# Linear attention with a mixture-of-experts layer: values ahead of state products in the first and last block pairs, and other moves in the order of the attention stage

## The chip, the cores and the metric

The kernel runs on one core of a Trainium2 chip. The metric is the time of one execution on the device in microseconds (us). The kernel before took 392.94 us as the median of three runs, which lay between 392.67 and 392.99 us.

A core has engines that work side by side and wait for one another through semaphores: PE (TensorE, matrix products; each of its products is preceded by a weight load), DVE (VectorE), ACT (ScalarE), POOL (GpSimd) and SP (SyncE, which here only issues transfers). Each engine works through its own instructions in order. Products land in PSUM, from which DVE and ACT read.

## The reference

Queries, keys and values have shape (4 batches, 8 heads, 768 positions, 64). The first half is linear attention with decay, computed in blocks; the second half sends each of the 3072 rows of 512 numbers to one of 8 experts.

```
for each block b of the sequence:
    intra = (q_b k_b^T) * Dmask          # Dmask[i,j] = lam^(i-j) for i >= j
    out_b = intra v_b + (q_b * lam^(pos+1)) kv_state
    kv_state = lam^block * kv_state + (k_b * lam^(block-1-pos))^T v_b
x = out as 3072 rows of 512
e = argmax(x w_gate + modality_bias);  p = its probability
out[row] = p * (relu(x[row] w1[e]) w2[e])
```

## The kernel before, in words

**Blocks.** The kernel takes blocks of 128 positions, so each batch has NC = 6 blocks and there are 24 blocks, g = 0 to 23. They are loaded in pairs: load(m) brings k, q, v and k by rows for blocks 2m and 2m+1, into one of four slots. A load into a used slot waits until the products that read it are done. The first two pairs come in four transfers each, so that PE can begin early.

**The steps of one block.** `scores(g)` (line 250) are 16 products on PE into the PSUM tile s; `mask(g)` multiplies them by the decay matrix dk on DVE and gives the tile pt. `query(g)` (line 218) makes q times the powers pq on POOL. `keys(g)` (line 226) makes the decayed keys kd, in 8 instructions on ACT, or in one on POOL where on_pool is set. `products(g)` (line 263) are 16 products on PE that make the block's share of the state, into one half of the PSUM tile kv: even blocks write its first half, odd blocks its second. `add(g)` (line 272) adds that share to the decayed state on DVE; for the first block of a batch it is one copy. `from_state(both)` (line 283) opens an output tile o for each block named and multiplies the state before the block by the decayed query; its products use half of the array's rows and half of its columns each, and where two blocks are named their products alternate. `values(g)` (line 294) adds pt times v to the same tile o, closes it, and copies it on ACT into xt, which gathers four blocks. The tile o has two buffers, s has two, kv has one.

**Turning and gating.** Four blocks in xt make a group. `turn(grp, tb)` transposes a quarter of it on PE into a buffer of o, and DVE and then ACT copy it out as rows. `gates(grp)` are 32 small products that give the routing scores. `turns(grp)` (line 333) is turn, turn, gates, turn, turn.

**The order.** For PE, DVE, ACT and SP the order of the instructions is the order in which the program calls them; nothing is moved. The opening (lines 813 to 856) is written out by hand for blocks 0 to 5. Then a loop runs over m = 2 to 11, called pass m here: with a = 2m and b = 2m+1 it does add(b), the scores, masks, keys and queries of blocks a+2 and b+2, some small routing steps, the state products and values of blocks a and b, then products(a+2), products(b+2), add(a+2), and in odd passes the four turns. Pass 2 handles block 5 alone, since the opening has already finished block 4. The loop begins thus:

```
for m in range(2, pairs):
    a, b = HB * m, HB * m + 1
    ahead = m + 1 < pairs
    add(b)
    ...
    if ahead:
        block(a + 2)
        mm = block(b + 2)
```

`keep_busy(n)` (line 788) issues n products whose result nobody reads. Small DVE steps (choosing the expert, the lists of tiles) are put into a list by `put`, and `do(n)` issues the next n of them. `tick(mm)` lets one scatter of finished rows go out on POOL after the product mm.

**The experts.** After the loop, wide tiles of 256 rows run through the experts (`first_layer`, `second`). Two thin tiles, of 64 and of 32 rows, are worked in between: `thin_second` (line 750) is a thin tile's second layer, its scaling on ACT and its output transfer by POOL. It is called inside the `first_layer` of the next wide tile through `finish`. The last wide tile's second layer ends the kernel.

Of the kernel before, what the change touches and what calls it, by code (L numbers as in the profile page):

```python
# [15 lines left out]
P = 128  # L16
B, H, S, D = 4, 8, 768, 64
NP = H // 2
# [25 lines left out]
def linear_attention_moe(tc, qkv, lam, modality, wg, mbias, w1, w2, out):  # L44
    nc = tc.nc
    with ExitStack() as ctx:
# [163 lines left out]
        def loaded(g):  # L210

            t = halves[g // HB][:, :, g % HB]
            kt, qt = (t[:, i].rearrange("p (a t) -> p a t", a=NP) for i in range(2))
            return kt, qt, t[:, 2], t[:, 3]
# [65 lines left out]
                                                   scalar=pq[:, p, P - 1 : P], in1=kp[:, g % HB, p, :],  # L280
                                                   op0=ALU.mult, op1=ALU.add)

        def from_state(both):

            for g in both:
                ops[g] = ps.tile([P, NP, P], F32, name="o", bufs=2)
            for p in range(NP):
                for g in both:
                    if g % NC > 0:
                        for hl, r in enumerate(halves2):  # L290
                            nc.tensor.matmul(ops[g][place(g, hl), p, :], state[g % NC % 3][r, p, :], qds[g][r, p, :],  # L291
                                             start=(p == 0), stop=False)

        def values(g):
            c = g % NC
            vt, op, pt = loaded(g)[2], ops.pop(g), pts.pop(g)
            for p in range(NP):
                for hl in range(2):
                    mm = nc.tensor.matmul(op[place(g, hl), p, :], vt[:, (2 * p + hl) * D : (2 * p + hl + 1) * D],  # L299
                                          pt[:, hl, p, :], start=(c == 0 and p == 0), stop=(p == NP - 1))  # L300
            if g % 4 == 0:
                xts[g // 4] = work.tile([P, NP, 4, 4, Q], F32, name="xt", bufs=2)
            nc.scalar.copy(out=xts[g // 4][:, :, :, ORDER.index(g % 4), :], in_=op.rearrange("p a (c t) -> p a c t", c=4))
            return mm

        groups = []
# [8 lines left out]
        def turn(grp, tb):  # L315
            tp = ps.tile([P, NP, P], F32, name="o", bufs=2)
            for p in range(NP):
                nc.tensor.transpose(out=tp[:, p, :], in_=xts[grp][:, p, tb].rearrange("k t a -> k (t a)"), identity=ident)  # L318
            row = row_tile(4 * grp + tb)[:, :DM].rearrange("t (p h d) -> t p h d", p=NP, h=2)
            tp = tp.rearrange("t p (h d) -> t p h d", h=2)  # L320
            half = P // 2
            nc.vector.tensor_copy(out=row[:half], in_=tp[:half])
            for h in range(2):
                nc.scalar.copy(out=row[half:, :, h], in_=tp[half:, :, 1 - h])

        def gates(grp):
            for p in range(NP):
                for t in range(4):
                    mm = nc.tensor.matmul(lps[t * Q : (t + 1) * Q, grp % 2, :], wgq[:, ORDER[t] % HB, p, :], xts[grp][:, p, :, t, :],
                                          start=(p == 0), stop=(p == NP - 1), tile_position=(0, t * Q))  # L330
            return mm

        def turns(grp):
            turn(grp, 0)
            turn(grp, 1)
            mm = gates(grp)
            turn(grp, 2)
            turn(grp, 3)
            return mm
# [102 lines left out]
        def count():  # L442

            nc.tensor.matmul(cp, onesb, ohsum, start=True, stop=True)
# [367 lines left out]

        keep_busy(9)
        decays()
        keys(0, True)
        scores(0)
        mask(0)
        keep_busy(5)
        lam_halves()
        powers()  # L820
        from_state((0,))
        values(0)
        block(1, True)
        products(0)
        add(0)
        block(2)
        keys(3)
        from_state((1,))
        values(1)
        products(1)  # L830
        add(1)
        scores(3)
        mask(3)
        query(3)
        products(2)
        gpsimd_constants()
        load(SLOTS)
        from_state((2,))
        values(2)
        add(2)  # L840
        products(3)
        from_state((3,))
        values(3)
        add(3)
        block(4)
        turn(0, 0)
        turn(0, 1)
        gates(0)
        block(5)
        turn(0, 2)  # L850
        turn(0, 3)
        load(1 + SLOTS)
        products(4)
        add(4)
        from_state((4,))
        values(4)
        for m in range(2, pairs):
            a, b = HB * m, HB * m + 1
            ahead = m + 1 < pairs
            add(b)  # L860
            if m == 4 or m == 8:
                routed = m // 4 - 1, *choose(m // 4 - 1, gate_rows())
# [3 lines that stand above are left out]
                if m > 4:  # L866
                    tick(mm)
            if m == 2:
                routing_constants()
            elif m == 3:  # L870
                clear(slice(E * CAP, E * CAP + TT), TT)
            do(9 if m % 4 == 0 else 8)
            if m > 2:
                from_state((a, b))
                values(a)
            else:
                from_state((b,))
            mm = values(b)
            if m == 5 or m == 9:
                jobs += [("slots", one_slot)] * RC  # L880
            if m > 4:
                tick(mm)
            if m + SLOTS < pairs:
                load(m + SLOTS)
            if ahead:
                for g in (a + 2, b + 2):
                    products(g)
                add(a + 2)
            if m == 4 or m == 8:
                ranks(routed[-1])  # L890
                slots += slots_of(*routed)
            elif m == 5:
                count()
                early = early_list("A", listA)
            elif m == 9:
                count()
                early = early_list("B", listB, early)
            elif m == 10:
                turn_rows(0)
            if m % 2 and ahead:  # L900
                mm = turns(m // 2)
                if m > 4:
                    tick(mm)
            else:
                do(4)
            if m == 8:
                need("slots")
                raw1 = w1_part("raw1", F32)
                fetch_w1(*fetch_regs(0, True))
                fetch_x(0)  # L910
            elif m == 9:
                raw2 = w2_part("raw2", F32)
                fetch_w2(*fetch_regs(0, True))
                fetch_x(1)
# [97 lines left out]
        for n in [3] + list(range(wides, fixed_ones)):  # L1012
            first_layer(between)
            between = lambda i: None
            thin = {wides + 1: thins, wides + 3: thins + 1}.get(n)
            if thin:
                thin_rows(thin)
            m = n + 1 if n > 3 else wides
            if m < fixed_ones:
                fetch_w2(*fetch_regs(m, m == wides))  # L1020
                turn_rows(m)
                split_rows()
                if m + 1 < fixed_ones:
                    fetch_x(m + 1)
                split_w1()
                if m + 1 < fixed_ones:
                    fetch_w1(*fetch_regs(m + 1))
            second(n, 0)
            if thin:
                hn = thin_first(xf[thin], homes[thin][0])  # L1030
            second(n, 1)
            if thin:
                hnt[thin] = thin_turn(hn)
                between = finish(thin, 0)
            thin = {wides: thins, wides + 2: thins + 1}.get(n)
            if thin:
                fetch_x(thin)
                fetch_w1(*fetch_regs(thin, True), to=homes[thin][0])
                fetch_w2(*fetch_regs(thin, True), to=homes[thin][1])
        ordered.close()  # L1040
        _, (more,) = nc.values_load_multi_w_load_instructions(
            nums[0:1, 0:1], engines=mybir.ALL_ENGINES, min_val=MIN_WIDE, max_val=MAX_WIDE, bass_reorder=False)
# [65 lines left out]
```

## Time and profile before

| what | value |
|---|---|
| runs | 392.67, 392.94, 392.99 us |
| the profiled execution | 393.13 us, of which the span from first to last instruction is 391.4 us |
| PE busy | 381.3 us, 97% of the span, 3602 products |
| DVE, ACT, POOL busy | 66%, 54%, 25% |
| PE in 40 slices of 9.8 us | 8, 9, 8, then 9 in each until the last, which is 3 |
| DMA busy in the same slices | 7 in the first, 9 in the next three, mixed after, 2 or less in most of the last ten |

The profile is of one execution on the core. An engine's busy time is the sum of its instructions. In a row of the timeline the first number is the start, the second how long the row lasts; "x16" says that 16 instructions are merged in it; a bracket says how long the engine was idle before it and which instruction ended that wait. Products are pipelined and their ends are modelled, so one row of PE may overlap the next by some hundredths of a microsecond.

### The profile page before, as it was taken

The page shows a single profiled execution, that of the slowest core. Times are in us where ns is not written, and L with a number is a line of the kernel's source. Part 1 is how long each engine was busy: PE and PEld are TensorE (multiplying, and loading weights), DVE is VectorE, ACT ScalarE, POOL GpSimd, SP SyncE. Part 2 cuts the span into 40 slices and gives each one's busy share as a digit, 9 for nine tenths or more (in the row PEclk, how much of TensorE's full clock was granted, in tenths as well). Part 3 has the DMA queues.
Part 4 walks back from the last instruction along what each step waited for, and adds up shares of the span by engine and source line. Part 5 has one row for each costly group of instructions (what it writes and reads, how often), then busy time and mean ns, then how long its engine had stood idle before and what let it go on. Part 6 is the DMA issues. An engine that isn't in the chain of part 4 may idle for free.

```text
span 391.4 us, 9713 instructions
## 1 busy us (share of the span) xinstructions
PE 381.3 (97%) x3602; PEld 337.5 (86%) x3602; DVE 256.8 (66%) x461; ACT 210.5 (54%) x411; POOL 98.3 (25%) x128
## 2 busy tenths in 40 slices
PE   8989999999999999999999999999999999999993
PEld 4879888898888989999898987889979899898982
DVE  6667779878577687875768574375764756668520
ACT  1558578675556564464746454355355554646520
POOL 1653218656411267020020102102012020201101
PEclk9999999999999999999999999999999999999998
DMA  7999977999759993399814999762950211200101
GB/s 250 388 402 338 360 253 288 383 345 329 232 147 287 332 336 147 140 371 307 245 55 119 289 405 305 269 194 63 337 175 30 56 54 26 56 28 3 55 2 51
DMA packets 42456, 82.72 MB, mean 211 GB/s; under 512 B 7326, under 2 KB 20126, under 8 KB 42400
## 3 DMA queue, kind: packets, MB, share of 16 engines
q1 hardware_dynamic: 38480, 69.23, 53.5%
q0 software_dynamic: 3920, 12.78, 8.5%
q8 instruction: 30, 0.49, 0.5%
q14 instruction: 26, 0.21, 0.2%
HBM read 89.52 MB, written 17.84 MB: 274 GB/s over the span
## 4 chain that ended last, share of the span: by engine, by line
PE 56%; issue 31%; POOL 4%; DMA 3%; DVE 3%; SPq 1%; ACT 1%; POOLq 0%; DVEq 0%
PE o L674 6%; PE o L676 6%; PE o L675 6%; PE s L255 5%; PE o L299 5%; POOL out_dram L718 4%; PE o L291 3%; PE kv L674 2%; PE s L676 2%; PE kv L675 2%; PE s L675 2%; PE s L674 2%; PE kv L676 2%; PE o L318 2%; DMA load<-in_qkv_dram 2%
## 5 line engine op out<-in xcount | busy, mean ns | idle before, releaser
L583 DVE TENSOR_TENSOR w2l<-raw,w2h 128x1024 fp32r<-128x1024 f32 x48 | 58.8, 1224 | 39.2 <-ACT w2h L582 38.1
L718 POOL DMA_INDIRECT out_dram<-y,idx x24 | 30.0, 1249 | 212.2 <-ACT y L717 188.2
L674 PE MATMUL o<-w2h,hh 128*128 128x512 f32 x192 | 75.4, 393 | 0.0
L676 PE MATMUL o<-w2h,hl 128*128 128x512 f32 x192 | 74.9, 390 | 0.0
L675 PE MATMUL o<-w2l,hh 128*128 128x512 f32 x192 | 74.8, 390 | 0.0
L583 DVE TENSOR_TENSOR w1l<-raw,w1h 128x1024 fp32r<-128x1024 f32 x44 | 51.5, 1220 | 2.0 <-ACT w1h L582 2.0
L582 ACT CAST w2h<-raw 128x1024 fp32r<-128x1024 f32 x48 | 49.9, 1039 | 0.0
L674 PE MATMUL kv<-xh,w1h 128*128 128x256 f32 x176 | 49.8, 283 | 0.0
L674 PE MATMUL s<-xh,w1h 128*128 128x256 f32 x176 | 49.6, 282 | 0.0
L675 PE MATMUL s<-xl,w1h 128*128 128x256 f32 x176 | 49.5, 281 | 0.0
L675 PE MATMUL kv<-xl,w1h 128*128 128x256 f32 x176 | 49.5, 281 | 0.0
L676 PE MATMUL s<-xh,w1l 128*128 128x256 f32 x176 | 49.5, 281 | 0.0
L676 PE MATMUL kv<-xh,w1l 128*128 128x256 f32 x176 | 49.5, 281 | 0.0
L582 ACT CAST w1h<-raw 128x1024 fp32r<-128x1024 f32 x44 | 42.9, 1046 | 0.0
L674 PEld LDWEIGHTS o<-w2h,hh 128*128 128x128 f32 x192 | 36.0, 188 | 7.8 <-issue 0.8
L676 PEld LDWEIGHTS o<-w2h,hl 128*128 128x128 f32 x192 | 36.1, 188 | 7.6
L675 PEld LDWEIGHTS o<-w2l,hh 128*128 128x128 f32 x192 | 36.1, 188 | 7.1
L717 ACT ACTIVATE y<-o,idx 128x512 f32<-128x512 f32 x24 | 16.4, 684 | 40.4 <-PE o L676 34.6
L237 ACT ACTIVATE kd<-load,dk 128x64 f32<-128x64 f32 x144 | 35.7, 339 | 3.5 <-DMA load<-in_qkv_dram 3.4
L674 PEld LDWEIGHTS kv<-xh,w1h 128*128 128x128 f32 x176 | 33.3, 189 | 0.6 <-issue 0.6
L674 PEld LDWEIGHTS s<-xh,w1h 128*128 128x128 f32 x176 | 33.2, 189 | 0.3
L675 PEld LDWEIGHTS s<-xl,w1h 128*128 128x128 f32 x176 | 33.2, 189 | 0.3
(190 smaller groups left out, 637.1 us busy)
## 6 DMA issues: line engine op xcount, KB each, us to landing
raw<-in_w_dram SPq DMA_DIRECT2D x96, 512.0 KB
load<-in_qkv_dram SPq DMA_DIRECT2D x6, 2048.0 KB
both<-in_w_dram SPq DMA_DIRECT2D x16, 512.0 KB
xg<-placed SPq DMA_DIRECT2D x48, 128.0 KB
placed<-blank SPq DMA_DIRECT2D x9, 528.0 KB
load<-in_qkv_dram SPq DMA_DIRECT2D x8, 512.0 KB
load<-in_qkv_dram SPq DMA_DIRECT2D x4, 1024.0 KB
load<-in_qkv_dram SPq DMA_DIRECT2D x4, 768.0 KB
```

Of the source, the lines that this page charges most:

```text
L237: nc.scalar.activation(out=kds[g][:, p, hl, :], in_=kn[:, p, hl, :], func=AF.Copy, scale=dk[:, hl, p, P - 1 : P])
L255: mm = nc.tensor.matmul(scs[g][:, hl, p, :], kt[r, p, :], qt[r, p, :], start=True, stop=True)
L291: nc.tensor.matmul(ops[g][place(g, hl), p, :], state[g % NC % 3][r, p, :], qds[g][r, p, :], start=(p == 0), stop=False)
L299: mm = nc.tensor.matmul(op[place(g, hl), p, :], vt[:, (2 * p + hl) * D : (2 * p + hl + 1) * D], pt[:, hl, p, :], start=(c == 0 and p == 0) ...
L318: nc.tensor.transpose(out=tp[:, p, :], in_=xts[grp][:, p, tb].rearrange("k t a -> k (t a)"), identity=ident)
L582: nc.scalar.copy(out=hi, in_=src)
L583: nc.vector.tensor_tensor(out=lo, in0=src, in1=hi.bitcast(F32), op=ALU.subtract)
L674: nc.tensor.matmul(out, ah, bh, start=first, stop=False)
L675: nc.tensor.matmul(out, ah, bl, start=False, stop=False)
L676: return nc.tensor.matmul(out, al, bh, start=False, stop=last)
L717: nc.scalar.activation(out=y, in_=yp, func=AF.Copy, scale=idx[:, t, 1:2].bitcast(F32))
L718: sc = nc.gpsimd.indirect_dma_start(out=out, out_offset=bass.IndirectOffsetOnAxis(ap=idx[:, t, 0:1], axis=0), in_=y, in_offset=None, bound ...
```

## The change

There are five edits.

1. A pair of blocks can now begin its output tiles with `values(g, begins=True)` and end them with `from_state(both, ends=True)`, which then copies both tiles out (`give`). Blocks 2 and 3, 4 and 5, and 22 and 23 are done so; 22 and 23 had been a pair before, in the other order.
2. In the opening `lam_halves` and `powers` stand ahead of the first mask, the five products of `keep_busy(5)` are gone, scores(1) stand ahead of products(0), the keys of block 1 are made on ACT, and load(4) is called ahead of scores(3) instead of behind products(2).
3. In the loop add(a+2) stands between products(a+2) and products(b+2). In odd passes products(b+2) stand inside `turns`, between the gates and the last two turns.
4. In odd passes four small steps (`do(4)`) and, in passes 5 and 9, the start of a list stand inside `turns` as well; the `do(4)` at the end of the even passes is gone, and the rows of a group are scattered one tick later.
5. The second thin tile's `thin_second` comes after the last wide tile.

```
+        def from_state(both, ends=False):
...
-                                             start=(p == 0), stop=False)
+                                             start=(p == 0 and not ends), stop=(ends and p == NP - 1))
+            if ends:
+                for g in both:
+                    give(g)
...
-        def turns(grp):
+        def turns(grp, amid):
             turn(grp, 0)
             turn(grp, 1)
             mm = gates(grp)
+            do(4)
+            amid()
             turn(grp, 2)
             turn(grp, 3)
...
         decays()
+        lam_halves()
+        powers()
         keys(0, True)
         scores(0)
         mask(0)
-        keep_busy(5)
-        lam_halves()
-        powers()
-        from_state((0,))
-        values(0)
-        block(1, True)
+        scores(1)
         products(0)
         add(0)
-        block(2)
-        keys(3)
+        values(0)
+        mask(1)
+        query(1)
+        keys(1)
         from_state((1,))
         values(1)
+        scores(2)
+        mask(2)
+        query(2)
+        keys(2)
         products(1)
         add(1)
+        load(SLOTS)
         scores(3)
         mask(3)
         query(3)
+        keys(3)
+        gpsimd_constants()
         products(2)
-        gpsimd_constants()
-        load(SLOTS)
-        from_state((2,))
-        values(2)
         add(2)
+        values(2, begins=True)
+        values(3, begins=True)
         products(3)
-        from_state((3,))
-        values(3)
+        from_state((2, 3), ends=True)
+        load(1 + SLOTS)
         add(3)
         block(4)
         turn(0, 0)
         turn(0, 1)
         gates(0)
-        block(5)
+        products(4)
         turn(0, 2)
         turn(0, 3)
-        load(1 + SLOTS)
-        products(4)
         add(4)
-        from_state((4,))
-        values(4)
+        block(5)
+        values(4, begins=True)
...
+            if m == 2:
+                mm = values(b, begins=True)
+                from_state((a, b), ends=True)
+            elif not ahead:
+                values(a, begins=True)
+                mm = values(b, begins=True)
+                from_state((a, b), ends=True)
+            else:
                 from_state((a, b))
                 values(a)
...
             if ahead:
-                for g in (a + 2, b + 2):
-                    products(g)
+                products(a + 2)
                 add(a + 2)
             if m == 4 or m == 8:
+                products(b + 2)
                 ranks(routed[-1])
...
-            if m % 2 and ahead:
-                mm = turns(m // 2)
+            elif m % 2 and ahead:
+                def amid():
+                    begin_list()
+                    products(b + 2)
+                mm = turns(m // 2, amid)
...
-            else:
-                do(4)
+            elif ahead:
+                products(b + 2)
...
-                between = finish(thin, 0)
+                if thin == thins:
+                    between = finish(thin, 0)
...
+        thin_second(thins + 1, hnt.pop(thins + 1), homes[thins + 1][1])
```

## Rows read from the trace of the kernel before

**Rows 1.** Windows: span and busy us of PE, PEld, DVE, ACT, POOL; clock, DMA, GB/s.

```profile
0.00:50.00 50.00, 46.77 (x750) 38.37 (x751) 33.09 (x80) 26.52 (x90) 19.95 (x44) 1.00 0.92 341
50.00:100.00 50.00, 49.36 (x937) 44.02 (x937) 40.45 (x128) 36.44 (x123) 27.38 (x36) 1.00 0.94 324
```

**Rows 2.** Timeline of PE, opening and pass 2: start, us, engine, line, operation, tiles.

```profile
1.29 4.02 PE L792 MATMUL o<-busy 128*128 128x512 bf16 x9 [1.29 <-DVE busy L100]
...
6.78 1.25 PE L792 MATMUL o<-busy 128*128 128x512 bf16 x5
...
11.27 1.16 PE L255 MATMUL s<-load 64*128 64x128 f32 x16 [0.28 <-DMA load<-in_qkv_dram]
12.36 1.09 PE L291 MATMUL o<-qd,state 64*64 64x128 f32 x16
...
28.05 1.09 PE L291 MATMUL o<-qd,state 64*64 64x128 f32 x16 [0.99 <-ACT grp L324]
...
30.09 2.06 PE L255 MATMUL s<-load 64*128 64x128 f32 x32
...
34.02 1.10 PE L269 MATMUL kv<-load,kd 128*64 128x64 f32 x32
```

**Rows 3.** Timeline of POOL, DVE and ACT in the opening.

```profile
7.21 1.06 POOL L233 TENSOR_TENSOR kd<-load,dk 128x512 f32<-128x512 f32 x1 [5.80 <-DMA load<-in_qkv_dram]
9.84 1.06 POOL L233 TENSOR_TENSOR kd<-load,dk 128x512 f32<-128x512 f32 x1 [1.58 <-DMA load<-in_qkv_dram]
8.50 1.37 DVE L128 TENSOR_TENSOR_SCAN pq<-lamq,nought 128x128 f32<-128x128 f32 x4
12.57 2.02 ACT L237 ACTIVATE kd<-load,dk 128x64 f32<-128x64 f32 x8 [2.66 <-DMA load<-in_qkv_dram]
```

**Rows 4.** Timeline of PE, passes 3 to 5.

```profile
39.86 1.10 PE L269 MATMUL kv<-load,kd 128*64 128x64 f32 x32
...
46.38 1.10 PE L291 MATMUL o<-qd,state 64*64 64x128 f32 x32
...
56.37 1.09 PE L318 MATMUL o<-ident,xt 128*128 128x128 f32 x8
```

**Rows 5.** Timeline of DVE, state steps of passes 2 and 3.

```profile
35.20 0.42 DVE L276 COPY state<-kv 128x256 f32<-128x256 f32 x1 [0.19 <-PE kv L269]
...
41.03 0.86 DVE L279 SCALAR_TENSOR_TENSOR state<-state,pq,kv 128x64 f32<-128x64 f32 x4 [2.25 <-PE kv L269]
```

**Rows 6.** Timeline of ACT, passes 4 and 5.

```profile
50.20 0.26 ACT L356 ACTIVATE l<-l 128x64 f32<-128x64 f32 x1 [2.30 <-DVE l L356]
...
55.27 1.06 ACT L303 COPY xt<-o 128x512 f32<-128x512 f32 x2
```

**Rows 7.** Timeline of DVE and PE, pass 6; eight small steps stand between its first two.

```profile
63.40 0.25 DVE L356 TENSOR_TENSOR geA<-x,thr 128x104 f32<-128x104 f32 x1
...
65.64 0.85 DVE L279 SCALAR_TENSOR_TENSOR state<-state,pq,kv 128x64 f32<-128x64 f32 x4
...
64.46 1.10 PE L269 MATMUL kv<-load,kd 128*64 128x64 f32 x32
```

**Rows 8.** Timeline of DVE, pass 8.

```profile
80.45 0.42 DVE L276 COPY state<-kv 128x256 f32<-128x256 f32 x1 [0.87 <-PE kv L269]
```

**Rows 9.** Timeline of PE, last pass.

```profile
95.34 1.66 PE L291 MATMUL o<-qd,state 64*64 64x128 f32 x32
```

**Rows 10.** Timeline of ACT: the last wide output and the second thin one.

```profile
385.18 0.69 ACT L717 ACTIVATE y<-o,idx 128x512 f32<-128x512 f32 x1 [4.75 <-PE o L676]
...
298.65 0.37 ACT L765 ACTIVATE yn<-o,idx 128x128 f32<-128x128 f32 x1 [1.26 <-PE o L761]
```

**Rows 11.** Source lines 718 and 766: output transfers, wide and thin, issue to landing.

```profile
DMA to landing us min/median/max: 2.7/3.3/8.7
...
DMA to landing us min/median/max: 2.3/2.3/2.3
```

**Rows 12.** Windows: the last stretch, columns as in rows 1.

```profile
388.00:391.40 3.40, 0.00 (x0) 0.00 (x0) 0.00 (x0) 0.00 (x0) 0.00 (x0) 0.54 0.12 45
```

More of the change, by code (lines that the diff above doesn't have):

```diff
@@ L281, in add, with out_tile, give @@
                                                    op0=ALU.mult, op1=ALU.add)
-        def from_state(both):
+        def out_tile(g):
+            if g not in ops:
+                ops[g] = ps.tile([P, NP, P], F32, name="o", bufs=2)
+            return ops[g]
+        def give(g):
+            if g % 4 == 0:
+                xts[g // 4] = work.tile([P, NP, 4, 4, Q], F32, name="xt", bufs=2)
+            nc.scalar.copy(out=xts[g // 4][:, :, :, ORDER.index(g % 4), :],
+                           in_=ops.pop(g).rearrange("p a (c t) -> p a c t", c=4))
+        def from_state(both, ends=False):
             for g in both:
-                ops[g] = ps.tile([P, NP, P], F32, name="o", bufs=2)
+                out_tile(g)
             for p in range(NP):
@@ L291, in from_state, with values @@
                             nc.tensor.matmul(ops[g][place(g, hl), p, :], state[g % NC % 3][r, p, :], qds[g][r, p, :],
-                                             start=(p == 0), stop=False)
-        def values(g):
-            c = g % NC
-            vt, op, pt = loaded(g)[2], ops.pop(g), pts.pop(g)
+                                             start=(p == 0 and not ends), stop=(ends and p == NP - 1))
+            if ends:
+                for g in both:
+                    give(g)
+        def values(g, begins=False):
+            vt, op, pt = loaded(g)[2], out_tile(g), pts.pop(g)
             for p in range(NP):
@@ L299, in values @@
                     mm = nc.tensor.matmul(op[place(g, hl), p, :], vt[:, (2 * p + hl) * D : (2 * p + hl + 1) * D],
[L300 to L303, printed above, removed]
+                                          pt[:, hl, p, :], start=((begins or g % NC == 0) and p == 0),
+                                          stop=(not begins and p == NP - 1))
+            if not begins:
+                give(g)
             return mm
@@ L848, in linear_attention_moe, with begin_list @@
         gates(0)
-        block(5)
+        products(4)
         turn(0, 2)
         turn(0, 3)
-        load(1 + SLOTS)
-        products(4)
         add(4)
-        from_state((4,))
-        values(4)
+        block(5)
+        values(4, begins=True)
+        early = None
+        def begin_list():
+            nonlocal early
+            if m == 5:
+                count()
+                early = early_list("A", listA)
+            elif m == 9:
+                count()
+                early = early_list("B", listB, early)
         for m in range(2, pairs):
@@ L872, in linear_attention_moe @@
             do(9 if m % 4 == 0 else 8)
-            if m > 2:
+            if m == 2:
[6 more added lines that the diff above has]
+            else:
                 from_state((a, b))
                 values(a)
-            else:
[L877 to L880, printed above, removed]
+                mm = values(b)
             if m > 4:
@@ L885, in linear_attention_moe @@
             if ahead:
-                for g in (a + 2, b + 2):
-                    products(g)
+                products(a + 2)
                 add(a + 2)
             if m == 4 or m == 8:
+                products(b + 2)
                 ranks(routed[-1])
                 slots += slots_of(*routed)
[L892 to L897, printed above, removed]
             elif m == 10:
+                products(b + 2)
                 turn_rows(0)
-            if m % 2 and ahead:
-                mm = turns(m // 2)
+            elif m % 2 and ahead:
[3 more added lines that the diff above has]
+                mm = turns(m // 2, amid)
+                if m == 5 or m == 9:
+                    jobs += [("slots", one_slot)] * RC
                 if m > 4:
                     tick(mm)
-            else:
-                do(4)
+            elif ahead:
+                products(b + 2)
             if m == 8:
```

## The prediction

> **What bounds the kernel now.** I read the page first, then windows, then the timelines of PE, DVE, ACT and POOL over the attention stage, then the tail. The page's slices show PE at 9 tenths or more from the fourth on. The windows show where PE has room: in the first 50 us it is busy 46.77, in the next 50 us 49.36 [rows 1]. So some 3.9 us can be had from PE's waits before the experts begin, over three of it in the opening; beyond that only work taken out of PE's stream, or a shorter tail, moves the end. Whatever the loop does to PE's order is paid or earned one for one, since the expert stage keeps PE full and gives nothing back.
>
> **The opening.** I count how far block 6's scores, at 30.09 now [rows 2], move.
>
> Out of PE's stream: the five busy products, 1.25. A state product for one block takes 1.09 [rows 2], one for two blocks 1.10 [rows 4], so a second block rides free. Less the overlap of merged rows, a single one is worth 1.03. Those of blocks 2, 3 and 4 go, one for the pair 2 and 3 comes, and block 4 rides with 5 later: 2.06. The waits of 0.28 and 0.99 [rows 2] go too, one because those scores come after their data, the other because block 4's state products no longer stand behind the turns. Together 4.58.
>
> Into it: scores(1) now follow scores(0), which end at 6.78. POOL waited for block 0's second transfer until 7.21 and for block 1's second until 9.84 [rows 3]; block 1's first, which the scores need, lies between, at about 8.5. That is 1.7 of waiting (0.4 to 3.1 by the two rows; I take the middle, as the parts are equal). Then ACT: values(0) end near 11.3 (8.5, plus 1.1 for scores, 0.55 for half a pair's products and 1.05 for values, which stream as many columns as a state product: an estimate). Behind them ACT has a copy of 0.53 (half of 1.06 [rows 6]), the keys of block 1 at 2.02 [rows 3], another copy and the keys of block 2: done at 16.5. PE reaches products(2) at 16.1 and waits 0.4. Two further waits, of the first turn for its copy and in handovers, I put at 0.4 (0.1 to 1.0). Together 2.5.
>
> The powers, 1.37 of scans [rows 3] and the small copies before them, now delay mask(0) to about 9.4; PE gets to values(0) at 10.3, which hides it; with scores(1) at the early bound PE would wait 0.4 there. Transfers: two parts took 2.63 [rows 3], so a pair of four parts takes 5.3 and the third pair after the first is in at about 25.6, an estimate; scores(6), asked for two microseconds earlier, still find it. load(4) and load(5) pass nothing on SP's queue that PE is short of, and wait for the same products as before.
>
> Net 4.58 - 2.5 = **2.05 earlier** (0.5 to 3.4).
>
> **Pass 2.** Here the new place of the state step bites. Rows 5 show state steps that begin only when the products of both blocks are done: the one of block 8 had DVE idle for 2.25 and began at 41.03, just after the pair of products ended at 40.96 [rows 4], though its own half was done half a microsecond earlier. The two halves of kv are ordered as one tile, so products(b+2), now behind add(a+2), wait until DVE has finished it. In pass 2 DVE's earlier work ended at 35.01 (35.20 less 0.19 idle [rows 5]); moved up by 2.05 it ends at 32.96. The first half of the products ends at 32.5 (34.02 [rows 2] less 2.05, plus half of 1.10). The copy of 0.42 ends at 33.38, the second half at 33.95, against 33.07 unhindered: **0.9 lost**. Queued behind it on PE is everything.
>
> **Odd passes.** Two microseconds of turns and gates lie between add(a+2) and products(b+2), which hides the step. The half product then fills the third turn's wait for ACT; but the first turn loses the half product that stood ahead of it. In passes 3, 7 and 9 I call that **0.1 earlier** each (-0.3 to 0.4). In pass 5 it costs. ACT waited until 50.20 for DVE, then had two copies, the keys of two blocks (4.0) and two more copies, the last done at 56.33 [rows 6]; the turn began at 56.37 [rows 4]. The chain moves up with PE, which now gets there half a microsecond sooner: **0.4 lost** (0 to 1.0).
>
> **Pass 6.** add(14) runs at 65.64, behind eight small steps begun at 63.40 [rows 7]. With the 0.85 left by then it ends at 65.64, so that the second half ends at 66.2; unhindered both would be done at 64.7 (64.46 plus 1.10 [rows 7], less 0.85). **1.5 lost**; none of it if DVE is through earlier, 2.0 if ACT's delay in pass 5 carries over.
>
> **Passes 8 to 11.** In pass 8 DVE idles 0.87 before its copy [rows 8], so the price is the copy, 0.42, and two handovers: **0.55 lost**. Passes 4 and 10 have no second product there. In the last pass the pair's state products take 1.66 [rows 9] against 1.10, since they wait for the state; values ahead of them cover it: **0.55 earlier**. The small steps and ticks that move lie on DVE and POOL beside PE's work; the first scatters end one tick later, with several passes to the fetch that needs them.
>
> **The tail.** The 32-row tile's second layer costs PE the same in either place. At the end ACT then has 0.37 to do in place of 0.69 [rows 10], and the transfer lands in 2.3 in place of 2.7 at the least, 3.3 in the median [rows 11]; with the queues empty I take 2.7. **0.7 earlier** (0.3 to 1.3).
>
> **The sum.** 2.05 - 0.9 + 0.3 - 0.4 - 1.5 - 0.55 + 0.55 + 0.7 = 0.25 earlier. The profiled execution took 393.13, its span 391.4 and 1.7 around it that stay; so 392.9 against its own time. The runs' median is 0.19 lower: **392.7**.
>
> **The rivals.**
>
> *The second products do not wait.* If PE may write one half of kv while DVE reads the other, or DVE is through by then, the 0.9, 1.5 and 0.55 vanish. Some 0.6 of the 2.95 comes back as DVE's or ACT's lateness in passes 5 to 7, so 390.4. For it: no row of before shows PE waiting for a state step. Against it: the 2.25 of rows 5. The Trainium skill (PSUM — Partial Sum Buffer, Terms) says that two engines on the same bank and quadrant at once is an error, which is a reason for such an ordering; by it this rival falls, but no run here shows a product that waits. Chance 0.28.
>
> *ACT becomes the bound of the turns: slower.* In passes 3, 5, 7 and 9 the first turn needs ACT's copy of the block just finished, with nothing ahead of it on PE now, and ACT has block 1's keys besides. If the copy is late by the half product (0.55) and its own 0.53 in each, the four cost 4.3, of which half can hide behind DVE's lateness in pass 6: 2.1 in place of the sum's 0.1, so 394.7. It decides once ACT's copies end after products(a+2). For it: the 0.04 between copy and turn in pass 5. Against it: elsewhere ACT has slack, as the 2.30 before its step in pass 4 shows [rows 6]. Chance 0.17.
>
> *The clock falls in the opening: slower.* The first nine busy products took 4.02, or 0.45 each; the five at 6.78 took 0.25 each [rows 2], so the first ran at 1.2 GHz and the later at 2.4. In the last stretch the granted clock averages 0.54 [rows 12], after PE had ended its work by 385.18 [rows 10]: idleness lowers it. The wait of 0.99 at 28.05 left it high, the products behind it taking the same 1.09 [rows 2]. The new 1.7 lies between. A stretch like the first costs 4.02 - 9 x 0.25 = 1.8, so 394.5; it decides where the wait for block 1 is long. The Trainium skill (TensorE: Matmul & The Clock Gate, Part 1) puts it as "the default state is throttled, and activity releases the throttle", which speaks against taking busy products out; the rows agree in that the first products ran at the lower level. Chance 0.08.
>
> **How the numbers follow.** The forecast has 0.47. Its own size is uncertain by about 1 us, mostly the opening and pass 6, so of it 0.31 lies within 0.2% (0.8 us, what a measurement here can tell), 0.09 below and 0.07 above. Faster: 0.09 and the first rival's 0.28, 0.37. Same: 0.31 and 0.04 from a mild form of ACT's, 0.35. Slower: 0.07, 0.13 and 0.08, 0.28. The range reaches to the rivals on both sides, 390.2 to 394.8; the forecast's own is 391.7 to 393.7.
>
> **What would show it.** Block 6's scores near 28.05; state products of blocks 2 and 3, 4 and 5 in rows of 32; in passes 2, 6 and 8 a PE wait ended by DVE's state step, the longest in pass 6; in pass 5 a turn that waits for ACT; no wait in the last pair; scores(1) in 1.2 for their 16 products, not in twice that; a last ACT step of 0.37. The forecast is wrong if PE shows no wait for the state step, or if the experts begin more than 1 us away from 0.45 later than before (the sum without its tail).

## The result, and the profile after

The changed kernel takes 397.97 us as the median of six runs (396.97 to 398.90), the kernel before 393.06 on the same chip; the ratio is 1.0116, with a 95% interval of 1.0088 to 1.0143. The change makes the kernel 5 us slower; the prediction was 392.7, no difference that can be measured. The profiled execution took 396.97, its span 395.2.

Line numbers are shifted in the changed kernels: there from_state is L302, values L312, a turn L331, and the small steps L371. Its windows, columns as in [rows 1]:

```profile
0.00:50.00 50.00, 45.17 (x772) 37.83 (x774) 34.52 (x84) 29.44 (x102) 19.17 (x43) 1.00 0.93 344
50.00:100.00 50.00, 44.26 (x819) 39.64 (x817) 38.23 (x97) 32.60 (x117) 23.60 (x29) 0.97 0.79 265
```

In the second window PE is busy 44.26 where it was 49.36 [rows 1]. The first window's 45.17 is no loss: its busy products are gone, and it holds 22 more products than before. The opening went better than forecast. PE's timeline, opening and pass 2, answering [rows 2]:

```profile
8.53 1.16 PE L255 MATMUL s<-load 64*128 64x128 f32 x16 [1.22 <-DMA load<-in_qkv_dram]
...
16.46 0.69 PE L269 MATMUL kv<-load,kd 128*64 128x64 f32 x16 [0.43 <-ACT kd L237]
...
27.40 2.06 PE L255 MATMUL s<-load 64*128 64x128 f32 x32
...
30.41 1.10 PE L302 MATMUL o<-qd,state 64*64 64x128 f32 x32
...
32.79 0.69 PE L269 MATMUL kv<-load,kd 128*64 128x64 f32 x16 [0.67 <-DVE state L276]
```

Block 6's scores begin at 27.40 against 30.09, 2.69 earlier. The new wait for block 1 is 1.22, and in pass 2 the second products wait 0.67 for the state copy. Then PE's timeline in passes 5 to 7, and the start of the experts, answering [rows 4, 7]:

```profile
54.89 1.09 PE L331 MATMUL o<-ident,xt 128*128 128x128 f32 x8 [0.53 <-ACT xt L291]
...
63.47 0.63 PE L269 MATMUL kv<-load,kd 128*64 128x64 f32 x16
68.22 1.12 PE L269 MATMUL kv<-load,kd 128*64 128x64 f32 x16 [4.11 <-DVE state L279]
69.27 3.08 PE L255 MATMUL s<-load 64*128 64x128 f32 x32
...
75.98 1.09 PE L331 MATMUL o<-ident,xt 128*128 128x128 f32 x8 [0.23 <-ACT xt L291]
```

The wait forecast at 1.5 in pass 6 is 4.11, and behind it the same kind of products takes 3.08 in place of 2.06 [rows 2]: that is the clock's lower level. DVE and POOL in pass 6 show why the state step is late:

```profile
62.58 0.25 DVE L371 TENSOR_TENSOR geA<-x,thr 128x104 f32<-128x104 f32 x1
...
63.51 3.19 DVE L371 TENSOR_TENSOR pastA<-sidx,sumsEA 128x16 f32<-128x16 f32 x1
...
67.23 0.85 DVE L279 SCALAR_TENSOR_TENSOR state<-state,pq,kv 128x64 f32<-128x64 f32 x4
```

```profile
62.94 1.19 POOL L430 DMA_INDIRECT placed<-grp,sloti  x1 [8.74 <-DVE geA L371]
64.16 2.49 POOL L222 TENSOR_TENSOR qd<-load,pq 128x512 f32<-128x512 f32 x2
```

One small step, over 16 columns, lasts 3.19 and ends at 66.70, as POOL ends its two queries at 66.65. The list's other small steps take 0.17 to 0.26 each. The state step, three steps later, is through at 68.08, and PE goes on at 68.22. The clock answers to no row of before; a window behind the wait:

```profile
68.00:72.00 4.00, 3.78 (x46) 3.69 (x48) 1.52 (x6) 0.00 (x0) 1.83 (x4) 0.57 0.99 325
```

The granted clock averages 0.57 there. The waits of PE, grouped:

```profile
PE kv L269 <- DVE state L279: 4.1, 1, 4.1
PE s L255 <- DMA load<-in_qkv_dram: 1.7, 2, 1.2
PE kv L269 <- DVE state L276: 1.3, 2, 0.7
...
PE o L331 <- ACT xt L291: 1.2, 4, 0.5
```

In the last pair the state products are 1.10 for 32, with no wait, against 1.66 [rows 9]. The experts begin at 103.91, and the tail, answering [rows 10], ends with the short step:

```profile
102.88 1.10 PE L302 MATMUL o<-qd,state 64*64 64x128 f32 x32
103.91 1.35 PE L709 MATMUL s<-xt,raw 128*128 128x256 f32 x5
```

```profile
390.12 0.37 ACT L780 ACTIVATE yn<-o,idx 128x128 f32<-128x128 f32 x1 [1.27 <-PE o L776]
```

The experts begin 5.07 later than before (98.84 there); the span is 3.8 longer.

### The profile page after: what moved, and what is told of

Its sections match the earlier page's. It is cut to its first block, busy times and chain, and to the rows that moved or that the text cites. A ratio compares the mean times of both kernels' runs of the same rounds, so it can differ in the third digit from the quotient of the medians.

```text
span 395.2 us, 9712 instructions
## 1 busy us (share of the span) xinstructions
PE 379.4 (96%) x3597; PEld 337.1 (85%) x3597; DVE 260.5 (66%) x461; ACT 212.3 (54%) x419; POOL 97.2 (25%) x127
## 4 chain that ended last, share of the span: by engine, by line
PE 50%; issue 33%; POOL 6%; DVE 5%; DMA 2%; ACT 2%; SPq 1%; POOLq 0%; DVEq 0%
PE o L689 6%; PE o L691 6%; PE o L690 6%; POOL out_dram L733 4%; PE s L255 3%; PE o L312 3%; PE o L331 3%; PE kv L689 2%; PE kv L690 2%; PE s L691 2%; PE s L690 2%; PE s L689 2%; PE kv L691 2%; DMA load<-in_qkv_dram 2%; PE s L709 2%
## 5 line engine op out<-in xcount | busy, mean ns | idle before, releaser
L237 ACT ACTIVATE kd<-load,dk 128x64 f32<-128x64 f32 x152 | 37.6, 338 | 0.2
L430 POOL DMA_INDIRECT placed<-grp,sloti x24 | 26.6, 1106 | 29.0 <-DVE geA L371 8.7
```

Of the source, the lines that this page charges most:

```text
L237: nc.scalar.activation(out=kds[g][:, p, hl, :], in_=kn[:, p, hl, :], func=AF.Copy, scale=dk[:, hl, p, P - 1 : P])
L430: sc = nc.gpsimd.indirect_dma_start(out=placed, out_offset=bass.IndirectOffsetOnAxis(ap=at, axis=0), in_=row, in_offset=None)
```

## The experiments

Each ratio is to the kernel before on the same chip; that took 393.13, 393.26, 395.39 and 393.33 in the four sets. In the third set (pass 6 filled; loop of before, filled opening) it took 2.1 to 2.3 more than in the others, so only ratios and differences within it count.

| kernel | us, median (range) | ratio, 95% interval |
|---|---|---|
| both products first | 392.03 (391.94 to 395.62) | 0.9960 (0.9927 to 0.9994) |
| steps behind | 394.47 (393.69 to 396.66) | 1.0025 (0.9995 to 1.0054) |
| queries first | 393.21 (392.37 to 394.71) | 0.9981 (0.9949 to 1.0013) |
| tail alone | 392.03 (391.83 to 393.70) | 0.9949 (0.9921 to 0.9977) |
| both first and queries first | 390.95 (389.38 to 392.16) | 0.9922 (0.9888 to 0.9956) |
| opening alone | 391.33 (390.22 to 394.37) | 0.9955 (0.9923 to 0.9987) |
| loop of before | 390.06 (388.58 to 390.85) | 0.9913 (0.9885 to 0.9941) |
| early scatter | 393.77 (393.59 to 396.04) | 1.0019 (1.0001 to 1.0038) |
| pass 6 filled | 399.06 (398.75 to 400.32) | 1.0097 (1.0073 to 1.0121) |
| loop of before, filled opening | 392.07 (390.43 to 394.00) | 0.9899 (0.9874 to 0.9925) |
| repaired | 389.42 (389.36 to 389.84) | 0.9896 (0.9878 to 0.9915) |
| loop of before, early scatter | 390.34 (390.13 to 390.49) | 0.9918 (0.9899 to 0.9936) |

**Both products first.** Undoes the new place of the second products in the even passes.

```
 products(a + 2)
+if m % 2 == 0:
+    products(b + 2)
 add(a + 2)
```

> The changed kernel, with products(b+2) back ahead of add(a+2) in the even passes. Theory 1 (the second products wait for the state step): the three waits of 0.67, 4.11 and 0.64 go, and with the long one the stretch at half clock, which costs about 1.5; some 1.4 come back in pass 7, where state products need the same late state. So about 5.5 less than the changed kernel's 398: 392.5, between 391 and 393. Theory 2 (the loss sits in the opening, the odd passes or the tail, and the wait only takes up slack): above 396.

The waits of 0.67, 4.11 and 0.64 are gone and 6 us with them. But DVE is still held up, now in another step, and PE pays in pass 7. DVE, then PE:

```profile
62.27 3.35 DVE L371 TENSOR_SCALAR deltaA<-ntA 128x8 f32<-128x8 f32 x1
```

```profile
66.92 1.09 PE L302 MATMUL o<-qd,state 64*64 64x128 f32 x28 [0.82 <-DVE state L279]
...
73.87 1.25 PE L331 MATMUL o<-ident,xt 128*128 128x128 f32 x8 [1.17 <-ACT grp L337]
```

Its experts begin at 98.84, as those of the kernel before: all that the opening gains is spent in the loop. The step that is stretched is a different one, with other operands; what is common is that POOL's scatter and queries run beside it (61.86 to 65.57 there).

**Steps behind.** Pass 6's eight small steps stand behind its state step.

```
-do(9 if m % 4 == 0 else 8)
+if m != 6:
+    do(9 if m % 4 == 0 else 8)
...
     add(a + 2)
+    if m == 6:
+        do(8)
```

> The changed kernel, with the eight small steps of pass 6 behind add(14) instead of ahead of it. Theory 1 (add(14) is late since it stands behind the small steps, of which one takes 3.19): the wait in pass 6 falls from 4.11 to about 0.95 (the state step's 0.85 and two handovers), the clock stays high: about 4.7 less than 398, 393.3 (392.5 to 394). Theory 2 (the state step is late for another reason, its own wait or its own slowness): the wait stays near 4, 397 to 399.

The wait in pass 6 is 1.07 in place of 4.11, the price of the order without DVE's lateness. The steps, issued later, are stretched there (1.10 and 1.55 beside POOL's queries), and pass 7 waits 1.31 for a row copy. Five runs, 393.7 to 393.9, lie inside the expected range; the other five, 395.05 to 396.66, put the median 1.2 us above the expected 393.3.

**Queries first.** The first scatter is held back by one place, so that POOL's two queries of pass 6 run ahead of it, beside the masks.

```
     jobs += [("slots", one_slot)] * RC
-if m > 4:
+if m > 5:
     tick(mm)
```

> The changed kernel without the tick in pass 5, so that on POOL the queries of blocks 14 and 15 stand ahead of the first scatter. Theory 1 (the small step of 3.19 was held up by POOL's scatter and queries that ran beside it): the queries run beside the masks, the step takes about 0.2, the wait in pass 6 falls to the 1.5 that was forecast, the clock stays high: 393.9 (393 to 395). Theory 2 (the step is slow by itself, or by what it waits for on DVE): it still takes about 3, time 397 to 399. If the scatter then meets the steps, the step takes 1 to 2 and the time lies between.

DVE, POOL and PE in pass 6:

```profile
60.29 2.34 DVE L261 TENSOR_TENSOR pt<-s,dk 128x1024 f32<-128x1024 f32 x2
...
63.49 0.18 DVE L371 TENSOR_TENSOR pastA<-sidx,sumsEA 128x16 f32<-128x16 f32 x1
```

```profile
59.96 2.55 POOL L222 TENSOR_TENSOR qd<-load,pq 128x512 f32<-128x512 f32 x2 [7.59 <-issue]
...
63.99 1.19 POOL L430 DMA_INDIRECT placed<-grp,sloti  x1 [1.34 <-ACT kd L237]
```

```profile
65.19 0.69 PE L269 MATMUL kv<-load,kd 128*64 128x64 f32 x16 [1.10 <-DVE state L279]
```

The same step is 0.18 with no POOL work beside it. So POOL's place, not DVE's own work, made the 3.19; it is worth 3 of the 4.11, and the clock's fall with it. Five runs, 392.4 to 392.5, lie below the expected range, and five between 393.9 and 394.7. The masks run at their usual 2.34 for two beside the queries, so not every step is stretched. The Trainium skill (SBUF — State Buffer, SBUF: two separate sides) says that DVE and GpSimd share one pair of ports, locked for a whole instruction, and that a DVE operation contends where it runs in a mode that uses both ports or, against a GpSimd operation that reads SBUF, where it has two inputs there. That fits these two rows: the masks read one input from PSUM, the stretched `pastA` both from SBUF. `deltaA`, stretched in the both-first version, has one input; whether it runs in such a mode no run shows. By the Trainium skill, whichever starts first keeps the pair for its instruction. In the changed kernel the scatter was first (62.94, the step 63.51), which agrees; but the step, begun before the queries (64.16), did not come in ahead of them either and ended only behind both.

**Early scatter.** In the changed kernel the tick holds the first scatter behind the last product of the gates, which ended at 56.99 (its rows and their places were ready by then), yet it began at 62.94. Here one scatter of blank rows runs early, to rows that nobody reads.

```
 gpsimd_constants()
+early_scatter()     # iota of row numbers, then one indirect_dma_start of blank
 products(2)
```

> The changed kernel plus one scatter of blank rows on POOL behind its constants, into rows that nobody reads, so that the first scatter of rows in pass 5 is not POOL's first. In the changed kernel that scatter had its last input at about 57 and began at 62.94, 1.8 after an instruction load had ended. Theory (the late start is the load of what a first scatter needs): the scatter begins near 57.5, the queries no longer meet the mask-time steps of DVE, pass 6 waits 1 to 1.5 in place of 4.11 and the clock stays; time 393.5 (392.8 to 394.5). Rival (the start is set by something else, such as the order of POOL's instructions): it still begins after 62, pass 6 waits about 4, time 397.

The gates, in the changed kernel and here, then POOL and PE here:

```profile
55.91 1.08 PE L342 MATMUL x<-xt,wgq 128*32 128x128 f32 x32
```

```profile
57.42 1.08 PE L348 MATMUL x<-xt,wgq 128*32 128x128 f32 x32
```

```profile
24.25 0.13 POOL L186 IOTA at<- 128x1 int32 x1
24.68 1.18 POOL L187 DMA_INDIRECT placed<-blank,at  x1 [0.29 <-POOL at L186]
...
59.44 1.03 POOL L436 DMA_INDIRECT placed<-grp,sloti  x1 [3.73 <-ACT grp L343]
61.45 2.51 POOL L228 TENSOR_TENSOR qd<-load,pq 128x512 f32<-128x512 f32 x2 [0.98 <-PE s L261]
```

```profile
66.81 0.69 PE L275 MATMUL kv<-load,kd 128*64 128x64 f32 x16 [1.20 <-DVE state L285]
...
101.04 3.72 PE L715 MATMUL s<-xt,raw 128*128 128x256 f32 x16
```

This execution's opening is 1.5 longer (see below); here the gates end at 58.50, and the scatter begins 0.94 behind them in place of 5.95. (The brackets of the two scatters name `geA` and ACT's copies of other rows, the last to end before them; neither is an input of the scatter.) Most runs are at 393.6 to 393.8, against 397.0 for the lower three of the changed kernel: 3.3 less, with the loop's order unchanged. The late first scatter is thus the first link of the chain. Why it was late is open. That it waited for a load of instructions is likely (8 KB arrive 1.8 ahead of it), but what delays that load no run shows. Being a run's first scatter is not enough: the early one, itself the first of its run, began 0.30 after its row numbers were made. It also makes POOL's stream longer ahead of the scatters of rows, and no run separates that from its being a scatter.

**Pass 6 filled.** Thirteen idle products in the 4.11.

```
+if m == 6:
+    keep_busy(13)
 products(b + 2)
```

> The changed kernel with 13 products that nobody reads between products(14) and products(15) in pass 6, where PE waited 4.11 for the state step; they take 3.2 of that wait and move nothing else. Theory (PE's idleness let the clock fall to half from 68.05 to 71.47): the granted clock stays at full speed behind the wait, scores(16) take 2.06 in place of 3.08 and products(15) 0.69 in place of 1.12, and the experts begin about 1.5 earlier, near 102.4; time 1.5 less than the changed kernel's, 395.5 where the opening keeps the clock. Rival (the clock would fall there anyway, or its fall costs nothing): 397.

PE:

```profile
68.23 0.69 PE L269 MATMUL kv<-load,kd 128*64 128x64 f32 x16 [0.28 <-DVE state L279]
68.85 2.06 PE L255 MATMUL s<-load 64*128 64x128 f32 x32
...
75.12 1.09 PE L331 MATMUL o<-ident,xt 128*128 128x128 f32 x8 [0.82 <-ACT xt L291]
```

The clock stays at 1.00, so PE's idleness had lowered it. But only 0.4 reaches the experts (103.51 against 103.91). By pass 7's state products 1.45 is gained (70.83 against 72.28); the turn in pass 7, which waits 0.82 for ACT in place of 0.23, takes 0.6 of it back, pass 8 (0.77 in place of 0.64) and the last pair another 0.45. These waits are this version's own: where pass 6 is shortened in another way (steps behind, queries first, early scatter) that turn waits 0.23 as in the changed kernel. The idle products write a tile of o, and the first of them waited 0.80 for ACT's copy; that this upsets the later copies is likely, not shown.

What the fall of the clock costs is read from two versions without it, from products(15) of pass 6 to the experts: 34.23 in queries first (65.19 to the row below) and in the early scatter (66.81 to 101.04), 35.69 in the changed kernel (68.22 to 103.91). The 1.46 more is what its slower products add, 0.43 in products(15) and 1.02 in the scores behind them.

```profile
99.42 3.72 PE L709 MATMUL s<-xt,raw 128*128 128x256 f32 x16
```

So the expected 1.5 was the right price, but this version did not gain it: its runs lie 3.4 to 4.9 above the median of before, those of the changed kernel 3.9 to 5.8, and the intervals of the two ratios overlap.

**Tail alone.** Edit 5 on the kernel before: `thin_second` of the second thin tile is called behind the last wide tile.

> The kernel before, with only the second thin tile's second layer moved to the end. Theory 1 (the forecast's term): 0.7 less, 392.3, from a last ACT step of 0.37 and a shorter last transfer. Rival: the products at the end cost what they cost inside and the transfer's end is the same, no difference, 393.0. Rival 2: taking them out of the wide tile's first layer also takes a stall away, over 1.2 less.

The gain is 1.1, more than the theory's 0.7, and 1.0 of it is in the span (390.4 against 391.4). This execution's experts began 0.33 later (99.17 against 98.84); counted from there, the last transfer is issued 0.44 earlier (at 386.27 against 386.38), and the end comes 4.2 behind that issue in place of 5.0.

**Opening alone.** The new opening, with loop, last pair and tail of before.

> Edit 1 for blocks 2 to 5 and edit 2 only: the new opening in front of the loop, turns and tail of the kernel before. Theory (the opening gains 2.7 and the loop of before has no wait for a state step): block 6's scores near 27.4, experts begin near 96.5 against 98.84, time 390.8 (390.2 to 391.5). Rival (the loop cannot take the gain, since ACT's copies or DVE's small steps are then late in passes 3 to 7): 392 to 393, with PE waits for xt or for the state in these passes.

Block 6's scores begin at 27.42, the experts at 96.64, 2.2 earlier than before, and the profiled run took 390.83: the loop of before takes the gain, less 0.5. The median is higher because the runs spread to 394.37.

**Loop of before.** The same with the change's last pair and tail.

> The whole change except for the loop's edits 3 and 4: new opening, last pair with values first, tail with the second thin tile last, and the loop's order of products, state steps, turns and scatters as in the kernel before. Theory: the opening-alone version less 1.1 for the tail and 0.55 for the last pair, so 389.2 (388.5 to 390). Rival (as for the opening alone): 390.5 to 391.5.

Its lowest run, 388.58, is inside the theory's range; its median, 390.06, is just above it. The profiled one (390.26) shows what it lost; that the others lost the same is inferred. Its windows, and those of the version with both repairs, which was profiled in the same condition, of 8 to 14 us:

```profile
8.00:14.00 6.00, 5.43 (x68) 4.86 (x70) 3.64 (x5) 1.15 (x4) 1.65 (x2) 0.72 1.05 391
```

```profile
8.00:14.00 6.00, 5.34 (x66) 4.73 (x68) 3.64 (x4) 1.05 (x4) 1.95 (x2) 0.72 1.06 392
```

The clock fell in the opening. In these two and in the early-scatter version the wait ahead of scores(1) was 1.54 to 1.68, and products(2) began at 17.95 to 18.17; in the changed kernel's profile it was 1.22, and 16.46. The length of the wait does not decide it alone. In queries first it was 1.64, and the clock stayed high:

```profile
8.41 1.16 PE L255 MATMUL s<-load 64*128 64x128 f32 x16 [1.64 <-DMA load<-in_qkv_dram]
...
16.44 0.69 PE L269 MATMUL kv<-load,kd 128*64 128x64 f32 x16 [0.43 <-ACT kd L237]
```

```profile
8.00:14.00 6.00, 5.59 (x94) 4.93 (x96) 3.57 (x5) 2.79 (x10) 1.58 (x2) 1.00 1.05 391
```

So of four profiled executions with a wait of 1.5 to 1.7 three lost the clock; the expectation of the filled opening below counts those three alone. What tells them apart is open.

**Both first and queries first.**

> The changed kernel with both repairs: in the even passes products(b+2) stand ahead of add(a+2), and in pass 5's turns no scatter goes out, so that POOL's two queries of pass 6 come ahead of the first scatter. Theory (the loss is the wait for the state step plus POOL's stretching of a DVE step): no wait of PE for a state step in pass 6 or 7, the small DVE step pastA under 0.3 us, and what the both-first version still waited for in pass 7 (0.82 for the state, 1.17 for a row copy) gone; experts begin near 97 against 98.84, time 390.2 (389.5 to 391). Rival (DVE or ACT is late in passes 5 to 7 whatever the order): 392, as the both-first version.

No wait for a state step is left, and no step is stretched in pass 6. The experts begin at 98.14 in this execution, 1.7 of it the opening's clock; the runs form two groups, 389.4 to 390.1 and 391.0 to 391.3, and one at 392.16.

**Loop of before, filled opening.** Five idle products stand in the wait for block 1.

```
 mask(0)
+keep_busy(5)
 scores(1)
```

> The version with the loop of before (opening, last pair and tail of the change) with five products that nobody reads put back ahead of scores(1), in PE's wait for block 1's keys and queries. Three of the profiled runs so far had a granted clock of 0.6 to 0.7 between 8 and 11 us behind that wait where it was 1.5 to 1.7 long, and products(2) at 18 in place of 16.5; those with 1.2 to 1.3 had not. Theory (that fall is what splits the times of all versions with the new opening in two groups 1.5 apart): the clock stays at full speed in the opening, the slower group goes, median 388.6 (388.3 to 389.2) with nothing but odd runs above 389.5. Rival (the split has another cause, or the five products push scores(1) back by their own 1.25): median 390, as the version without them.

Inconclusive. The clock is 1.00 from 5 to 14 us and products(2) begin at 16.38, as expected, but the runs still spread, over 3.6 us. The profiled one, the longest, shows DVE idle for 2.46 before a state step whose products had long ended (65.22), and PE stopped in the same microsecond with no releaser. What that is stays open.

**Repaired.** The changed kernel with the even passes' products together, the queries ahead of the scatter, and the five idle products: the three edits above.

> The changed kernel with three repairs: products of both blocks ahead of the state step in the even passes, queries of pass 6 ahead of the first scatter, and five products that nobody reads in PE's wait ahead of scores(1). Without the last one its times lay in two groups, 389.4 to 390.1 and 391.0 to 391.3, and its profile, of the second group, had half the clock behind that wait. Theory (the fall of the clock in the opening makes the second group): full clock between 8 and 14 us, products(2) near 16.4, most runs in the lower group, 3.3 to 3.7 less than the kernel before on the same chip (389.6 where that takes 393.1), and single odd runs such as the kernel before has too. Rival (the groups have another cause): both groups as before, median 2.2 to 2.5 less.

The opening, and the experts' start:

```profile
8.00:14.00 6.00, 6.00 (x97) 4.94 (x97) 3.59 (x5) 2.77 (x10) 1.60 (x2) 1.00 1.05 390
```

```profile
16.46 0.69 PE L269 MATMUL kv<-load,kd 128*64 128x64 f32 x16 [0.43 <-ACT kd L237]
...
96.43 3.72 PE L709 MATMUL s<-xt,raw 128*128 128x256 f32 x16
```

All six runs lie between 389.36 and 389.84, 3.9 below the kernel before: there is no second group. No version without the five products was run on this chip, so the chip's part in that is not excluded; the full clock from 8 to 14 us, as in the other two versions with the five products, speaks for them. By the ratios this beats both kernels, by 1.0% and 2.2%.

**Loop of before, early scatter.** The filled opening and the early scatter.

> The loop of before with opening, last pair and tail of the change, five products that nobody reads ahead of scores(1), and one early scatter of blank rows on POOL behind its constants. In the version without the early scatter the first scatter of rows had its last input at 54.0 and began at 58.54, and POOL's later scatters and queries stretched DVE's small steps. Theory: the first scatter begins near 55 (the opening's clock kept: near 53.5), the steps are not stretched in pass 6, but PE did not wait for them there, so the time stays: 4.5 to 4.8 less than the kernel before (388.5 where that takes 393.1). Rival (the late scatter still costs PE, in passes where a wait came and went between executions): up to 0.5 less than that, and fewer odd runs.

The first scatter begins at 54.13, the small steps are 0.15 to 0.26, and the experts begin at 96.03, 0.4 before those of the repaired version; yet the end is later by 0.6, and the runs are 3.0 below the kernel before where 4.5 to 4.8 was expected. The expert stage, from there to the last output transfer's issue, takes 288.1 in place of 287.1. The changed kernel with the early scatter has the same 288.1, and no other version more than 287.8: the early scatter comes with a longer expert stage. Why is open.

## Why the prediction was wrong

The step that failed is the term of pass 6, "1.5 lost". The mechanism was right (the second products wait for the state step, the longest wait in pass 6), but the wait is 4.11, and the clock that it lets fall adds 1.45. The term took DVE's eight small steps at their durations from [rows 7]. I looked at which queues the scatter stood in, and called scatters and ticks work "beside PE's", without asking what they do to DVE when they land beside its small steps. In the kernel before the scatter went at 59.43 and its queries ended at 64.63, and one step was stretched to 0.68, to just behind that end; with both products ahead of the state step nobody paid for it. With POOL's work out of the way the term holds: in queries first pass 6, from scores(14) to scores(16), is 1.32 longer than before.

Measured from where a pass's scores begin to where the next pass's do, the changed kernel differs from the kernel before as follows. The rows for pass 6 and 7, before:

```profile
59.66 2.06 PE L255 MATMUL s<-load 64*128 64x128 f32 x32
...
65.49 2.06 PE L255 MATMUL s<-load 64*128 64x128 f32 x32
...
74.46 2.06 PE L255 MATMUL s<-load 64*128 64x128 f32 x32
```

and after, with the row of 69.27 above between them:

```profile
58.67 2.06 PE L255 MATMUL s<-load 64*128 64x128 f32 x32
...
79.26 2.06 PE L255 MATMUL s<-load 64*128 64x128 f32 x32
```

- **Opening**, 2.05 earlier forecast: 2.69, inside its bounds. The wait for block 1 was 1.22 where I took 1.7. But the third rival, with a chance of 0.08, is real too: in part of the executions the clock falls behind this wait and costs 1.5 to 1.7, where I had priced it at 1.8. The upper three of the changed kernel's runs lie 1.4 to 1.9 above the lower three. That these are such executions is inferred from the other versions with the new opening, since the profile of the changed kernel is of the other kind.
- **Pass 2**, 0.9 lost: 1.05, of it 0.67 the wait. **Pass 5**, 0.4: 0.50. **Pass 8**, 0.55: 0.87, of it 0.64 the wait. **Passes 10 and 11**, 0.55 earlier: 0.71.
- **Pass 6**, 1.5 lost: 4.77, and another 1.02 in pass 7 from the scores at the lower clock. Of the 4.77, 0.43 is products(15) at that clock.
- **Passes 3, 7, 9**, 0.1 earlier each: but for the clock 0.0, 0.0 and 0.1 later. The first turn waits 0.23 for ACT's copy in each; in the kernel before one turn of each of these passes waited 0.20 to 0.23 for ACT too. The second rival, ACT as the bound, is no more than that.
- **First rival**, second products don't wait: false; they wait in passes 2, 6 and 8.
- **Tail**, 0.7: 1.1 by the runs of tail alone, 1.2 by the traces, inside its bounds. The landing was 2.2 to 2.3, and I had taken 2.7.
- **The sum**: -2.69 + 1.05 + 0.50 + 4.77 + 1.02 + 0.87 - 0.71, and 0.26 in the other passes, make the 5.07 measured at the experts' start. Without pass 6 and the clock that is 0.72 earlier, where these terms of the forecast made 1.05: the opening's 0.64 more covers most of what the passes lost beyond their terms, so that this part comes out so near is partly luck.

## What to carry to other kernels

Before a wait on one engine's small steps is put into the path, look at what its neighbour runs beside them: a 0.17 us step cost 3 us because a scatter and two multiplications on POOL ran at the same time, and moving POOL's work by one place was enough. An order in which a late engine costs less is worth keeping (here both products ahead of the state step: DVE's lateness then cost waits of 0.82 and 1.17 in place of 4.11). Where a wait takes the place of filler products, check the clock in several executions: one profile may show the execution that kept it.

## What the runs showed of the hardware

- A DVE step that elsewhere takes 0.18 took 3.19 when it began beside a scatter and two multiplications on POOL; two masks beside two such multiplications took their usual 2.34.
- The first scatter of rows began 5.95 after the product that held it had ended, the same one behind an early scatter 0.94 after. The early scatter, itself the first of its run, began 0.30 after its row numbers.
- Waits of 0.93 to 1.27 before scores(1) left the clock at 1.00; of four waits of 1.54 to 1.68 three were followed by 0.72 on average from 8 to 14 us and one, of 1.64, by 1.00. One in the middle of the loop of 4.11 was followed by 0.57 over 4 us.
- The last thin transfer on POOL ends the span 4.2 to 4.4 after its issue (5.7 and 5.8 in the third set), the wide one 4.9 to 5.0.
